# Wider filler products in TensorE's opening gaps of an attention and two-expert kernel

## The chip, the core and the metric

The program runs on one core of a Trainium2 chip. The metric is the time of one execution on the device in microseconds. The kernel before took 1256.15 us in the median of three runs (1255.62 to 1256.72).

## The reference

Three stages, all in float32:

```
q_n = q / sqrt(mean(q*q) + 1e-6) * g_q          # k likewise; q, k, v: 4 x 12 x 448 x 64
attn = softmax(q_n @ k_n.T / 8);  x = attn @ v   # then tokens x 768: 1792 x 768
h = x @ w_in;  g = where(h > 0, h, exp(min(h, 0)) - 1);  x = g @ w_out        # 768 -> 2048 -> 768
xn = x / sqrt(mean(x*x) + 1e-6) * rms_g
out = (silu(xn @ w_gate) * (xn @ w_val)) @ w_out2                              # 768 -> 1536 -> 768
```

## The kernel before, in words

Two heads make a pair; there are 24 pairs, six for each of the four batches. For a pair, TensorE makes seven score tiles of 128 queries by 448 keys, VectorE takes their maxima (`nm`), ScalarE their exponentials (`p`, `pj`), TensorE turns the exponentials and multiplies them by v. The outputs of a batch feed the experts, whose weight products fill TensorE for the rest of the span. A float32 operand is mostly split into a high and a low part, so that one exact product is three products in a reduced format (`qh`, `ql` for queries and keys, in `gbig` for every second pair).

The first pairs have a special start. For pairs 0 and 1, queries are turned by TensorE against the identity (`turned_q`, 16 instructions as the profile counts them); for pairs 0 to 3, keys are first multiplied by their norm factor on GpSimd or VectorE, then turned by TensorE in four instructions (`turned_k`). `gains` multiplies the two gain vectors on GpSimd and turns the product on TensorE into a column `gsc` in the tile `small`, which the keys' split needs. So the start of pair 0 is one chain: query turn, gains, norm factor on VectorE, key multiplication on GpSimd, key turn, split on ScalarE (`qh`) and VectorE (`ql`), score tiles.

Nothing is issued as it is written down: `Plan.add` records each operation with an estimated price for each engine that can do it, `Plan.schedule` simulates all engines and picks an order, and `Plan.issue` writes the instructions out in that order. Each engine then runs its own list strictly in that order. In `issue` (line 292), TensorE's list gets filler: where the plan foresees TensorE idle before a product, products of a constant column `onef` (in `small`) with itself are put in, until their summed estimated price reaches the foreseen start. Their result is never read. Their weights are a full 128 by 128 tile that is loaded anew for each. Eight PSUM banks hold results; banks 0 to 3 are the score ring (`r_s`), so the fourth score bank is `bank3`. The filler's target, its width and its estimated price are set in `IDLE`, `idle_price` and `idle`; `plan.first_use` is the plan's first operation that writes the bank named in `plan.idle_bank`.

All instructions carry one source line of a helper (353) in the profile, so the rows are told apart by tile names and shapes. `small` as the input of a matmul is the filler. One float32 filler product appears as two instructions on TensorE and two weight loads.

Of the kernel before, what the change touches and what calls it, by code (L numbers as in the profile page):

```python
# [20 lines left out]
P = 128  # L21
# [12 lines left out]
class Plan:  # L34
# [15 lines left out]
    ACT_LAT = (2.8, 4.6)  # L50
    FLIGHT = 8
    BEGIN = 0.7
    IDLE = (1.2, 0.3, 4.6, 29.0, 0.125)

    def __init__(self, second):
        self.ops = []
# [234 lines left out]

    def issue(self):
        order, eng = self.schedule()
        t, used = self.IDLE[0], self.start_t[self.first_use]
        for i in order:
            if eng[i] == "pe" and t < self.IDLE[3]:
                late = self.start_t[i] >= used
                while t + self.IDLE[1] + self.idle_price(t, late) < self.start_t[i]:
                    self.idle(late)
                    t += self.idle_price(t, late)  # L300
                t = max(t, self.start_t[i] + self.ops[i][0]["pe"][0])
            self.ops[i][0][eng[i]][1]()

    def idle_price(self, t, late):
        cold = t < self.IDLE[2]
        if late:
            return self.IDLE[4] * (2 if cold else 1)
        return 0.43 if cold else 0.225


def k_tile_order(cd, cf1, cf2):
# [17 lines left out]
def kernel(ctx: ExitStack, tc: tile.TileContext, dims, tok, qk, vr, gq, gk, wst, rmsg, ident_in, out):  # L329
    nc = tc.nc  # L330
    B, H, S, D, CF1, CF2 = dims
# [23 lines left out]
    T, V, A, G, SP = (Engine(e) for e in (nc.tensor, nc.vector, nc.scalar, nc.gpsimd, nc.sync))  # L355
# [3 lines left out]
    plan = Plan(second)  # L359
# [38 lines left out]
    def size(ap):  # L398
        n = 1
        for s in ap.shape[1:]:  # L400
            n *= s
        return n
# [123 lines left out]
    gsc, eps, onef = (small[:, k:k + 1] for k in range(3))  # L526
# [72 lines left out]
    r_more = [r_rsb.t[0], r_xf.t[0]]  # L599
    banks = [pp.tile([P, 512], F32, name=f"bank{k}") for k in range(8)]  # L600
    r_s, r_t, r_o, r_m = Ring(), Ring(), Ring(), Ring()
    plan.idle_bank = banks[5].name
    def idle(late):
        o = banks[3][:, S + 1:512] if late else banks[5][:, 0:P]
        T.matmul(o, onef.to_broadcast([P, P]), onef.to_broadcast([P, size(o)]), start=True, stop=True)

    plan.idle = idle

    def phase(k):
        if k == 2:  # L610
# [1111 lines left out]
```

## Time and profile before

| | before |
|---|---|
| median of three runs | 1256.15 us |
| profiled execution | 1257.65 us |
| its span, first to last instruction | 1255.8 us |
| TensorE products busy | 1236.0 us (98%) |
| VectorE, ScalarE, GpSimd busy | 914.3, 708.1, 841.4 us |
| fillers: instructions, busy | 210, 44.7 us, all before 62 us |

The profile is that of one execution. Busy time of products is taken from modelled ends, so the start of the next instruction is the better clock for what one costs in a row of equals. A releaser behind an arrow is what ended the idle time ahead of a row.

### The profile page before, as it was taken

What the parts mean: (1) busy time and instruction counts of PE and PEld (TensorE: products, weight loads), DVE (VectorE), ACT (ScalarE), POOL (GpSimd) and SP (SyncE); (2) the same over time, 40 slices, a digit from 0 to 9 for tenths busy, and PEclk for the clock granted to TensorE, in tenths of its full rate; (3) what the DMA queues carried; (4) which work ended last, traced back from release to release, by engine and by line L of the source; (5) the groups of instructions that cost most, each with busy time, mean ns of one, the idle gap of its engine ahead of it and who ended that gap; (6) DMA issues with size and microseconds to landing.
All of it is one profiled execution on the core that took longest, in us unless ns stands there. A gap on an engine that the chain in (4) does not pass through costs nothing.

```text
span 1255.8 us, 18990 instructions
## 1 busy us (share of the span) xinstructions
PE 1236.0 (98%) x6400; PEld 1043.9 (83%) x6400; DVE 914.3 (73%) x1521; ACT 708.1 (56%) x1443; POOL 841.4 (67%) x729
## 2 busy tenths in 40 slices
PE   9989999999999999999999999999999999999998
PEld 9745787787877787777898999899999989999997
DVE  2387789887945458964489699966585699667677
ACT  1399677876865558765566365666363763322121
POOL 0155877887874658554897698975574788567583
PEclk9899999999999999999999999999999999999999
DMA  2157878776643448784669799675563246876866
GB/s 99 64 178 256 265 255 297 251 259 210 192 153 119 129 137 273 255 256 149 219 245 349 255 330 348 238 229 184 171 201 123 76 146 205 234 220 186 229 206 196
DMA packets 119270, 263.43 MB, mean 210 GB/s; under 512 B 15359, under 2 KB 58629, under 8 KB 119173
## 3 DMA queue, kind: packets, MB, share of 16 engines
q1 hardware_dynamic: 89364, 203.68, 48.2%
q0 software_dynamic: 21168, 49.55, 13.8%
q10 hardware_dynamic: 8640, 8.99, 2.6%
q8 instruction: 50, 0.82, 0.3%
q14 instruction: 48, 0.39, 0.1%
HBM read 181.01 MB, written 81.16 MB: 209 GB/s over the span
## 4 chain that ended last, share of the span: by engine, by line
PE 80%; DVE 9%; ACT 5%; DMA 2%; issue 2%; POOL 1%; SPq 0%; DVEq 0%; ACTq 0%; POOLq 0%
PE bank L353 80%; DVE bank L353 2%; DVE tbig L353 1%; ACT tbig L353 1%; DVE ybig L353 1%; ACT p L353 1%; POOL w L353 1%; ACT pt L353 1%; DVE wc L353 1%; DVE wt L353 1%; DMA bout_A<-w 1%; DVE late L353 1%; DVE xs L353 1%; DMA wr<-wst 1%; ACT ybig L353 1%
## 5 line engine op out<-in xcount | busy, mean ns | idle before, releaser
L353 PE MATMUL bank<-xs,w 128*128 128x448 f32 x1731 | 400.5, 370 | 0.8 <-POOL xs L353 0.4
L353 PE MATMUL bank<-gbig,w 128*128 128x448 f32 x1603 | 359.7, 369 | 3.2 <-DVE tbig L353 1.7
L353 PEld LDWEIGHTS bank<-xs,w 128*128 128x128 f32 x1731 | 318.3, 188 | 32.6 <-issue 5.7
L353 PEld LDWEIGHTS bank<-gbig,w 128*128 128x128 f32 x1603 | 296.2, 188 | 34.1 <-issue 5.5
L353 POOL TENSOR_TENSOR w<-wc,w 128x768 fp32r<-128x768 f32 (+1 forms) x103 | 191.9, 1864 | 46.4 <-ACT w L353 40.9
L353 PE MATMUL bank<-late,w 128*128 128x448 f32 x647 | 163.5, 366 | 0.3 <-DVE late L353 0.3
L353 DVE TENSOR_REDUCE bank<-bank 128x1 f32<-128x448 f32 x168 | 98.8, 623 | 60.6 <-PE bank L353 60.2
L353 PEld LDWEIGHTS bank<-late,w 128*128 128x128 f32 x647 | 121.4, 188 | 11.2 <-DVE late L353 1.0
L353 ACT ACTIVATE p<-bank,nm,rr 128x448 f32<-128x448 f32 x126 | 90.5, 722 | 31.6 <-DVE nm L353 25.9
L353 DVE SCALAR_TENSOR_TENSOR wc<-wc,wt 128x768 int32<-128x768 int32 x68 | 95.7, 1407 | 15.1 <-ACT wc L353 8.1
L353 POOL TENSOR_SCALAR w<-wc 128x768 fp32r<-128x768 f32 (+1 forms) x55 | 49.6, 902 | 71.8 <-PE bank L353 56.6
L353 ACT ACTIVATE pt<-bank 128x384 f32<-128x384 f32 (+2 forms) x174 | 75.0, 452 | 28.3 <-PE bank L353 25.4
L353 ACT ACTIVATE tbig<-bank 128x448 f32<-128x448 f32 x86 | 46.5, 543 | 66.1 <-PE bank L353 47.6
L353 PE MATMUL bank<-ident,p 128*128 128x128 f32 x441 | 69.8, 278 | 2.7 <-ACT pt L353 1.7
L353 ACT ACTIVATE w<-wc 128x768 fp32r<-128x768 f32 (+1 forms) x69 | 53.9, 782 | 31.4 <-PE bank L353 25.2
L353 PEld LDWEIGHTS bank<-ident,p 128*128 128x128 f32 x441 | 53.3, 141 | 21.2 <-ACT pt L353 5.2
L353 DVE TENSOR_TENSOR ybig<-bank,ybig 128x448 f32<-128x448 f32 x72 | 44.3, 619 | 34.6 <-PE bank L353 34.4
L353 ACT ACTIVATE wt<-wr 128x768 uint16<-128x768 uint8 x50 | 54.5, 1091 | 26.0 <-DVE wc L353 17.8
L353 DVE TENSOR_SCALAR wt<-wr 128x768 uint16<-128x768 uint16 x68 | 67.9, 998 | 0.7 <-DMA wr<-wst 0.5
L353 DVE TENSOR_TENSOR tbig<-bank,tbig 128x448 f32<-128x448 f32 x93 | 56.6, 619 | 16.1 <-PE bank L353 12.6
L353 POOL TENSOR_TENSOR w<-p,w 128x768 fp32r<-128x768 f32 x28 | 54.3, 1942 | 17.8 <-ACT w L353 17.6
L353 DVE TENSOR_TENSOR bank<-bank,tbig 128x448 f32<-128x448 f32 x58 | 36.4, 627 | 26.9 <-ACT tbig L353 13.6
(277 smaller groups left out, 2330.7 us busy)
## 6 DMA issues: line engine op xcount, KB each, us to landing
wr<-wst SPq DMA_DIRECT2D x68, 768.0 KB
wc<-kept SPq DMA_DIRECT2D x64, 384.0 KB
kept<-wc SPq DMA_DIRECT2D x52, 384.0 KB
w<-bgv_S POOLq DMA_DIRECT2D x38, 384.0 KB, 4.1
bgv_A<-w SPq DMA_DIRECT2D x36, 384.0 KB
bgv_S<-w SPq DMA_DIRECT2D x32, 384.0 KB
w<-bgv_A POOLq DMA_DIRECT2D x28, 384.0 KB, 4.2
rw<-qk SPq DMA_DIRECT2D x19, 512.0 KB
```

What stands on the lines that cost most here:

```text
L353: return lambda *a, **k: f(*[real(x) for x in a], **{n: real(x) for n, x in k.items()})
```

## The change

The filler gets one form instead of two: 128 columns into the first 128 columns of `bank3`, until the first planned operation that writes `bank3`, with estimated prices of 0.43 us (to 4.6 us of planned time) and 0.225 us (after). Before, it was 63 columns into the columns 449 to 511 of `bank3` from the first use of `bank5` on, with estimated prices of 0.25 and 0.125 us, and it could go on to 29 us of planned time. No other operation changes, and the order of all the others is the same on every engine.

```
-    IDLE = (1.2, 0.3, 4.6, 29.0, 0.125)
+    IDLE = (1.2, 0.3, 4.6)
...
-        t, used = self.IDLE[0], self.start_t[self.first_use]
+        t, end = self.IDLE[0], self.start_t[self.first_use]
...
-            if eng[i] == "pe" and t < self.IDLE[3]:
-                late = self.start_t[i] >= used
-                while t + self.IDLE[1] + self.idle_price(t, late) < self.start_t[i]:
-                    self.idle(late)
-                    t += self.idle_price(t, late)
+            if eng[i] == "pe" and t < end:
+                while t + self.IDLE[1] + self.idle_price(t) < self.start_t[i] and t < end:
+                    self.idle()
+                    t += self.idle_price(t)
...
-    def idle_price(self, t, late):
-        cold = t < self.IDLE[2]
-        if late:
-            return self.IDLE[4] * (2 if cold else 1)
-        return 0.43 if cold else 0.225
+    def idle_price(self, t):
+        return 0.43 if t < self.IDLE[2] else 0.225
...
-    plan.idle_bank = banks[5].name
-    def idle(late):
-        o = banks[3][:, S + 1:512] if late else banks[5][:, 0:P]
-        T.matmul(o, onef.to_broadcast([P, P]), onef.to_broadcast([P, size(o)]), start=True, stop=True)
-
-    plan.idle = idle
+    plan.idle_bank = banks[3].name
+    plan.idle = lambda: T.matmul(banks[3][:, 0:P], onef.to_broadcast([P, P]), onef.to_broadcast([P, P]), start=True, stop=True)
```

TensorE's list from the start of the program to the first score tile, before (`tk0` holds pair 0's queries and keys, `rsb1` the gains, `bank0<-qh` is the first score product):

```order
L353 MATMUL bank3_130<-small_63 128x63 x47
L353 MATMUL bank4_131<-ident_61,tk0_99 64x64 x2
L353 MATMUL bank4_131<-ident_61,tk0_99 64x128 x6
L353 MATMUL bank6_133<-ident_61,rsb1_125 128x1
L353 MATMUL bank3_130<-small_63 128x63 x34
L353 MATMUL bank6_133<-ident_61,tk0_99 128x128 x4
L353 MATMUL bank3_130<-small_63 128x63 x11
L353 MATMUL bank0_127<-qh_102 128x448
```

The same stretch of the changed kernel:

```order
L349 MATMUL bank3_130<-small_63 128x128 x26
L349 MATMUL bank4_131<-ident_61,tk0_99 64x64 x2
L349 MATMUL bank4_131<-ident_61,tk0_99 64x128 x6
L349 MATMUL bank6_133<-ident_61,rsb1_125 128x1
L349 MATMUL bank3_130<-small_63 128x128 x18
L349 MATMUL bank6_133<-ident_61,tk0_99 128x128 x4
L349 MATMUL bank3_130<-small_63 128x128 x6
L349 MATMUL bank0_127<-qh_102 128x448
```

The three batches of 47, 34 and 11 fillers are now batches of 26, 18 and 6, each twice as wide; what stands between them has not moved.

TensorE's list behind pair 0's last score tiles, before (`gbig` holds pair 1's split queries and keys):

```order
L353 MATMUL bank1_128<-ql_103,qh_102 128x448
L353 MATMUL bank2_129<-ql_103,qh_102 128x448
L353 MATMUL bank3_130<-small_63 128x63 x6
L353 MATMUL bank3_130<-gbig_88 128x448 x3
L353 MATMUL bank3_130<-small_63 128x63 x7
L353 MATMUL bank0_127<-gbig_88 128x448
L353 MATMUL bank1_128<-gbig_88 128x448
```

The same stretch of the changed kernel:

```order
L349 MATMUL bank1_128<-ql_103,qh_102 128x448
L349 MATMUL bank2_129<-ql_103,qh_102 128x448
L349 MATMUL bank3_130<-gbig_88 128x448 x3
L349 MATMUL bank0_127<-gbig_88 128x448
L349 MATMUL bank1_128<-gbig_88 128x448
```

The 6 and the 7 fillers around pair 1's first score tile are gone, and with them every filler after the first use of the fourth score bank by a score tile. In all, 105 fillers of 63 columns become 50 of 128.

## Rows read from the trace of the kernel before

**Rows 1.** The page's first part: busy us, share of span, instructions.

```profile
PE 1236.0 (98%) x6400; PEld 1043.9 (83%) x6400; DVE 914.3 (73%) x1521; ACT 708.1 (56%) x1443; POOL 841.4 (67%) x729
```

**Rows 2.** Timeline, TensorE: start us, us, work, idle before and releaser.

```profile
1.06 20.31 PE L353 MATMUL bank<-small 128*128 128x63 f32 x94 [1.06 <-DVE small L353]
...
21.30 1.96 PE L353 MATMUL bank<-ident,tk 64*64 64x64 f32 x16
...
23.19 0.58 PE L353 MATMUL bank<-ident,rsb 1*128 1x1 f32 x2
...
23.70 14.77 PE L353 MATMUL bank<-small 128*128 128x63 f32 x68
...
38.27 1.06 PE L353 MATMUL bank<-ident,tk 128*128 128x128 f32 x4
...
39.12 4.79 PE L353 MATMUL bank<-small 128*128 128x63 f32 x22
...
43.67 0.72 PE L353 MATMUL bank<-qh 128*128 128x448 f32 x1
...
44.19 0.57 PE L353 MATMUL bank<-qh,ql 128*128 128x448 f32 x1
...
44.56 0.57 PE L353 MATMUL bank<-ql,qh 128*128 128x448 f32 x1
...
46.49 1.88 PE L353 MATMUL bank<-ident,wr 64*64 64x64 f32 x16
...
48.60 0.37 PE L353 MATMUL bank<-qh,ql 64*128 64x448 f32 x2
...
48.80 0.36 PE L353 MATMUL bank<-ql,qh 64*128 64x448 f32 x2
...
52.66 1.55 PE L353 MATMUL bank<-small 128*128 128x63 f32 x12 [1.30 <-ACT p L353]
...
54.02 0.84 PE L353 MATMUL bank<-gbig 128*128 128x448 f32 x3
...
55.58 3.25 PE L353 MATMUL bank<-small 128*128 128x63 f32 x14 [0.72 <-DVE nm L353]
...
58.76 1.49 PE L353 MATMUL bank<-gbig 64*128 64x448 f32 x6
```

**Rows 3.** Timeline, the other engines and SyncE's queue.

```profile
7.12 0.45 DVE L353 TENSOR_SCALAR ones<-ident 128x128 fp32r<-128x128 f32 x1
...
26.65 1.05 POOL L353 TENSOR_TENSOR tk<-tk,rr 128x512 f32<-128x512 f32 x1 [19.16 <-DVE rr L353]
...
39.41 0.33 SPq L353 DMA_DIRECT2D tk<-tok  x1
...
40.09 0.75 DVE L353 SCALAR_TENSOR_TENSOR ql<-bank,small,qh 128x512 fp32r<-128x512 f32 x1 [10.96 <-ACT qh L353]
...
48.41 0.60 ACT L353 ACTIVATE gbig<-bank 128x512 fp32r<-128x512 f32 x1 [1.56 <-PE bank L353]
...
55.62 0.72 ACT L353 ACTIVATE p<-bank,nm,rr 128x448 f32<-128x448 f32 x1 [0.72 <-DVE nm L353]
...
59.06 0.72 ACT L353 ACTIVATE tbig<-bank,nm,rr 128x448 f32<-128x448 f32 x1 [2.62 <-DVE nm L353]
...
61.97 0.27 ACT L353 ACTIVATE rt<-bank 7x128 f32<-7x128 f32 x1 [1.20 <-PE bank L353]
```

**Rows 4.** Windows: stretch, us, busy (instructions), PEclk, DMA share, GB/s.

```profile
12.00:39.00 27.00, 27.00 (x134) 26.42 (x135) 5.07 (x15) 2.49 (x3) 1.05 (x1) 1.00 0.00 1
50.00:55.00 5.00, 3.26 (x23) 2.31 (x21) 4.05 (x10) 4.87 (x14) 1.88 (x2) 1.00 0.42 127
55.00:62.00 7.00, 6.42 (x29) 5.29 (x31) 2.74 (x9) 2.56 (x6) 0.00 (x0) 0.51 0.14 51
62.00:120.00 58.00, 52.65 (x322) 28.65 (x323) 46.32 (x115) 56.01 (x147) 32.32 (x30) 1.00 0.65 208
```

**Rows 5.** Groups by line and shape, TensorE, 0 to 62 us.

```profile
L353 PE MATMUL bank<-small 128*128 128x63 f32 x210 | 44.7, 413 | 3.1 <-ACT p L353 1.3 <-DVE small L353 1.1 <-DVE nm L353 0.7
```

## The prediction

> **What bounds the kernel now.** The page's first part comes first: TensorE's products are busy 1236.0 of 1255.8 us [rows 1], so whatever stands on TensorE is on the path, useful or not. The groups of TensorE then show what of it is filler: 210 instructions, 105 products of 63 columns, 44.7 us, with almost no idle time among them [rows 5]. The timeline of TensorE shows where they stand: two batches fill 1.06 to 21.30 and 23.70 to 38.27, a third 39.12 to 43.67, and only then comes the first score product [rows 2]. The other engines' rows show that they waited for TensorE and not the other way: GpSimd idled 19.16 us before pair 0's key multiplication, VectorE 10.96 us before the key split, SyncE issued its next load at 39.41 only [rows 3], and from 12 to 39 us the DMA engines moved nothing and VectorE was busy 5.07 of 27 us [rows 4]. So the opening is bound by filler that lasts longer than the gap it is to fill.
>
> Why it does: 47 products take 20.24 us to the next instruction, 34 take 14.57, 11 take 4.55, that is 0.431, 0.429 and 0.414 us each. The 6 at 52.66 take 1.36, or 0.227 us each [rows 2]. The two prices are the two levels of TensorE's clock: products of 448 columns start 0.37 us apart at 44.19 and 0.20 us apart at 48.60 [rows 2], 1.2 and 2.4 GHz. The clock column reads 1.00 already from 12 to 39 us [rows 4], against these spacings; I go by the spacings. So all of the first 43 us ran at 1.2 GHz, and the clock rose in the dense 448-column work after 43.67. From 55 to 62 us the column shows the low level itself, 0.51, and the 7 fillers there take 3.18 us, 0.454 each [rows 2, 4].
>
> From 62 to 120 us ScalarE is the bound, 56.01 of 58 us busy [rows 4]; behind that TensorE is full. Both follow from what came before, so time taken out of the opening should stay out.
>
> **The change part by part.** The order on all engines but for the filler is untouched. I follow pair 0's chain.
>
> First batch, 47 to 26 products. A 128-column product is not in the trace. Its price: the gains product moves one column with full 128-column weights, and its two instructions last from 23.19 to 23.70, 0.25 us each, no less than a filler's two at 0.216 each [rows 2]. So the number of columns does not set the price at 63 columns; the weight load does, and I take 0.431 us at the low and 0.227 us at the high level for 128 columns too. The other end is a price that grows in proportion to the columns, 0.876 and 0.461 us. Next, the clock. The 63-column filler did not raise it in 42 us; behind the 448-column work it rose between 44.56 and 48.60 [rows 2]. I take the 128-column filler to be like that work, and the rise to come as early in it as there, by 4.9 us: 9 products at 0.431 (to 4.94 us), 17 at 0.227, so the batch ends at 8.8 us instead of 21.30: 12.5 us less. Ends: all 26 at 0.431 give 12.3 us; all at 0.227 give 7.0, but the identity is only seen in use at 7.12 [rows 3], which the query turn needs too.
>
> Query turn and gains: 21.30 to 23.70, 2.40 us at the low level. At the high one half would be 1.2; pair 1's turn, in which the clock was rising, took 1.88 as against 1.96 [rows 2], so the columns are not all of it. I take 2.0, between 1.2 and 2.4. The gains start at about 10.3, the second batch at 10.8.
>
> Second batch, 34 to 18: 18 x 0.227 = 4.1 us, to 14.9 instead of 38.27. Here another wait is close behind. The key turn needs GpSimd's key multiplication, which ended at 27.70, 4.51 us after the gains started at 23.19 [rows 2, 3]; that chain on VectorE and GpSimd does not depend on the clock, so it ends at 10.3 + 4.5 = 14.8. Filler and chain come out together, and cheaper filler would give nothing more here.
>
> Key turn and third batch: four turns, 0.85 us before, 0.45 at the high level, to 15.35; 6 x 0.227 = 1.36, to 16.7. The second score product needs the key split, which ended at 40.84, 2.57 us after the key turn began [rows 2, 3]; less 0.4 for the faster turn that is 14.9 + 2.17 = 17.1. The second score product started at 44.19: 27.1 us less. I count 27.
>
> Score tiles at the high level: from 43.67 to ScalarE's copy of pair 1's turned queries at 48.41 pass 4.74 us, most at the low level [rows 2, 3]. ScalarE waited 1.56 us for TensorE there. Two score groups and one turn at 2.4 GHz need about 3.5. I take 1.2 us, with ends 0 and 2.4. From here on ScalarE sets the pace.
>
> The 13 late fillers: they stood in gaps, but pair 1's score tiles stood behind them, 1.36 us for the first and 3.18 us for the second group [rows 2], 4.54 in all. The gain can't be more than ScalarE's idle time there, 0.72 + 2.62 + 1.20 = 4.54 us [rows 3], by chance the same sum. It is not less than nothing, unless the clock suffers (the last rival). I take 3, as VectorE's maxima are then the next to be waited for.
>
> Sum: 27 + 1.2 + 3 = 31.2 us. The span of 1255.8 becomes 1224.6. The profiled execution took 1257.65, so 1226.5 in its terms; the median lies 1.5 below it, which gives 1225.0. The other way round, by TensorE's own load: 1236.0 less 44.7 of filler, plus 9 x 0.431 + 41 x 0.227 = 13.2, is 1204.5 busy; with the old idle time of 19.8 the span is 1224.3. The two agree.
>
> The Trainium skill speaks against my price. Its page "TensorE: Matmul & The Clock Gate", part 3 (packing small matmuls), says that a weight load overlaps matmuls in flight only where they use different rows of the array; a filler and its load use all of them. By that rule each filler would pay its columns on top of its load, and the time would go towards the first rival's. The trace disagrees in sum: products and loads are busy 1236.0 and 1043.9 us within 1255.8 [rows 1], so most loads did run beside products.
>
> **The rivals.** First, the price grows with the columns. For it: no row has this product. Against it: the one-column product. At proportional prices, with the clock up at 5 us, the first batch ends at 14.9 (21.5 x 0.461 after 5 us), the second at 16.9 + 8.3 = 25.2, the first score product comes at 28.4, 15.2 us less; with 1.2 and 3 the gain is 19.4, the time 1237.
>
> Second, the clock does not rise for 128-column filler either. For it: 92 fillers in a row did not raise it before. Then 26 x 0.431 ends at 12.3, the turn at 14.7, 18 x 0.431 at 22.4, key turn 0.85, 6 x 0.431 to 25.9; the first score product is 17.8 us earlier, the late part stays 3 and the score tiles give nothing: 20.8 less, 1235.
>
> Third, slower than before: without the late fillers the clock falls during the sparse opening and stays low through the stretch bound by ScalarE. From 62 to 120 us TensorE is busy 52.65 of 58 us at clock 1.00 [rows 4]. At 1.2 GHz this work needs 105.3 us, 47 more than the stretch; less the 31 won that is 16 us slower, 1272. It decides from the point where the low level holds some 70% of the stretch (0.7 x 52.65 - 5.35 of idle time = 31.5). For it: the clock did fall in the sparse stretch up to 55 us, where products were busy 3.26 of 5 us [rows 2, 4]. Against it: it fell although six fillers stood there, and the column is back at 1.00 from 62 on, after TensorE was busy 6.42 of 7 us [rows 4]; work at half speed fills the engine by itself. The same page of the Trainium skill, under "HAM oscillation", has the general form of this rival: gaps between bursts put the clock back to half. The fall at 55 us agrees; that the filler prevents it, no run here shows.
>
> Fourth, the gain is lost further on, to a transfer that comes no earlier. For it: DMA share 0.65 from 62 to 120 us. Against it: SyncE's first new load was issued 1.1 us after the key turn [rows 2, 3], so the loads move with the chain. If half were lost, 1240.
>
> **How the numbers follow.** What a measurement can tell here is about 0.2%, 2.5 us. Chances: the forecast 0.84, price by columns 0.05, clock not rising 0.05, slower 0.03, gain half lost 0.02, no change 0.01. The forecast's own range is 1220 to 1230: 1219.6 from the high ends of the score tiles and the late fillers (2.4 and 4.5) with another 2.7 from a batch that ends at 7.1 and a quicker turn; 1230 with nothing for the score tiles and little for the late ones. The first two rivals end at 1235 and 1237, so 1220 to 1236 leaves out under 0.2. Faster 0.95, within 0.2% 0.02, slower 0.03.
>
> **What would show it.** The first turn of pair 0 on TensorE at about 9 us (12 if the clock stays low, 15 if columns cost), the key turn at 15, the second score product at 17, fillers 0.43 us apart at first and 0.23 us later. ScalarE's waits of 0.72 and 2.62 us before pair 1's exponentials gone or much smaller. TensorE busy near 1204 us, and the stretch after the opening the same as before, only 31 us earlier. I am wrong if the fillers' spacing at the high level is well over 0.23 us, if the clock column shows the low level beyond the opening, or if TensorE waits for DMAs behind 30 us that it didn't wait for before.

## The result and the profile after

| | before | changed |
|---|---|---|
| median | 1256.43 us (4 runs, 1255.62 to 1257.88) | 1229.15 us (4 runs) |
| profiled execution, its span | 1257.65, 1255.8 us | 1227.55, 1225.7 us |
| ratio, 95% interval | | 0.9774 (0.9749 to 0.9799) |

One of the four runs of the changed kernel was disturbed (1951.49 us, mean granted clock 0.557); it counts in the median of 1229.15 but not in the ratio, and the median of the other three (1226.34, 1227.55 and 1230.75) is 1227.55. By the ratio the change makes the kernel 2.3% faster, 28 us (25.3 to 31.5 by the interval), against 31 forecast; both medians lie in the forecast's own range of 1220 to 1230. Run again twice, on other occasions, the changed kernel took 1224.51 and 1226.24 us in the median, 33.7 and 31.8 us less than the kernel before beside it.

First the page's part on engines (busy us, share of span, instructions), to be held against [rows 1].

```profile
PE 1204.2 (98%) x6290; PEld 1011.7 (83%) x6290; DVE 910.9 (74%) x1521; ACT 708.4 (58%) x1443; POOL 839.6 (68%) x729
```

TensorE lost 110 instructions and 31.8 us of busy time; the other engines have as many instructions as before, and their busy time differs by 3.4 us at most. TensorE is still 98% busy: what went was work on the path that served nothing.

Next the changed kernel's timeline, TensorE alone (start us, us, work, idle before and releaser), as in [rows 2].

```profile
1.06 7.71 PE L349 MATMUL bank<-small 128*128 128x128 f32 x52 [1.06 <-DVE small L349]
...
8.70 1.14 PE L349 MATMUL bank<-ident,tk 64*64 64x64 f32 x16
...
9.77 0.38 PE L349 MATMUL bank<-ident,rsb 1*128 1x1 f32 x2
...
10.07 4.28 PE L349 MATMUL bank<-small 128*128 128x128 f32 x36
...
14.31 0.66 PE L349 MATMUL bank<-ident,tk 128*128 128x128 f32 x4
...
14.80 1.50 PE L349 MATMUL bank<-small 128*128 128x128 f32 x12
...
16.06 0.45 PE L349 MATMUL bank<-qh 128*128 128x448 f32 x1
...
16.34 0.37 PE L349 MATMUL bank<-qh,ql 128*128 128x448 f32 x1
...
23.45 1.27 PE L349 MATMUL bank<-gbig 128*128 128x448 f32 x4 [1.30 <-ACT p L349]
...
25.74 1.48 PE L349 MATMUL bank<-gbig 64*128 64x448 f32 x5 [1.03 <-ACT p L349]
```

The query turn starts at 8.70 instead of 21.30, the key turn at 14.31 instead of 38.27, the second score product at 16.34 instead of 44.19. 18 fillers take 4.24 us to the key turn, which waited a little for the key product; their own instructions start 0.112 us apart, 0.223 a filler. The first 26 take 7.64 us, in which both levels of the clock occur. The query turn lasts 1.07 us instead of 1.89: it ran at the high level from the start.

The other engines of the same execution, as in [rows 3].

```profile
13.21 1.05 POOL L349 TENSOR_TENSOR tk<-tk,rr 128x512 f32<-128x512 f32 x1 [5.76 <-DVE rr L349]
...
15.72 0.75 DVE L349 SCALAR_TENSOR_TENSOR ql<-bank,small,qh 128x512 fp32r<-128x512 f32 x1
...
19.16 0.59 ACT L349 ACTIVATE gbig<-bank 128x512 fp32r<-128x512 f32 x1
...
25.58 0.72 ACT L349 ACTIVATE p<-bank,nm,rr 128x448 f32<-128x448 f32 x1
...
26.29 0.73 ACT L349 ACTIVATE tbig<-bank,nm,rr 128x448 f32<-128x448 f32 x1
...
28.95 0.27 ACT L349 ACTIVATE rt<-bank 7x128 f32<-7x128 f32 x1 [0.95 <-PE bank L349]
```

GpSimd's key product ends at 14.26, and the key turn starts 0.05 us later. ScalarE's waits of 0.72 and 2.62 us ahead of pair 1's exponentials are gone; the wait of 1.20 ahead of `rt` is 0.95. The clock in windows of the same lengths as in [rows 4] (stretch, us, busy of PE, PEld, DVE, ACT, POOL, PEclk, DMA share, GB/s):

```profile
20.00:25.00 5.00, 3.34 (x19) 1.98 (x18) 4.90 (x11) 4.98 (x15) 2.62 (x3) 1.00 0.32 100
25.00:32.00 7.00, 6.26 (x27) 4.66 (x28) 4.57 (x14) 5.57 (x15) 0.00 (x0) 0.51 0.39 117
32.00:90.00 58.00, 52.81 (x326) 28.84 (x324) 46.23 (x111) 55.10 (x141) 33.84 (x30) 1.00 0.64 212
```

The clock falls in the sparse stretch at 25 us and is back from 32 on, as it fell at 55 and was back at 62 before. The low level lasts 6.8 us in both, with the late fillers and without them.

To follow the lead through an execution, one instruction of ScalarE that all kernels have is taken as a mark: the squares of a later pair's queries and keys. First before, then after, from the timeline of ScalarE:

```profile
83.15 1.00 ACT L353 ACTIVATE tk<-tk 128x960 f32<-128x960 f32 x1
```

```profile
50.84 1.00 ACT L349 ACTIVATE tk<-tk 128x960 f32<-128x960 f32 x1
```

At the mark the lead, that is how much earlier the instruction comes than before, is 32.31 us. At the end of the span it is 30.1.

### The profile page after: what moved, and what is told of

Its sections match the earlier page's. It is cut to its first block, busy times and chain, and to the rows that moved or that the text cites. A ratio compares the mean times of both kernels' runs of the same rounds, so it can differ in the third digit from the quotient of the medians.

```text
span 1225.7 us, 18769 instructions
## 1 busy us (share of the span) xinstructions
PE 1204.2 (98%) x6290; PEld 1011.7 (83%) x6290; DVE 910.9 (74%) x1521; ACT 708.4 (58%) x1443; POOL 839.6 (68%) x729
## 4 chain that ended last, share of the span: by engine, by line
PE 77%; DVE 9%; ACT 6%; DMA 4%; issue 2%; POOL 2%; ACTq 0%; SPq 0%; DVEq 0%; POOLq 0%
PE bank L349 77%; DVE tbig L349 2%; DVE bank L349 2%; ACT tbig L349 1%; DMA scr<-rr 1%; ACT p L349 1%; ACT pt L349 1%; DMA rsb<-rsum 1%; DMA wr<-wst 1%; ACT ybig L349 1%; DVE ql L349 1%; DVE ybig L349 1%; DVE gbig L349 1%; POOL w L349 0%; DMA bout_A<-w 0%
## 5 line engine op out<-in xcount | busy, mean ns | idle before, releaser
L349 DVE SCALAR_TENSOR_TENSOR wc<-wc,wt 128x768 int32<-128x768 int32 x68 | 89.3, 1314 | 16.1 <-ACT wc L349 9.1
L349 ACT ACTIVATE pt<-bank 128x384 f32<-128x384 f32 (+2 forms) x174 | 75.1, 453 | 30.1 <-PE bank L349 27.3
L349 DVE TENSOR_SCALAR wt<-wr 128x768 uint16<-128x768 uint16 x68 | 71.4, 1050 | 1.4 <-DMA wr<-wst 1.2
L349 DVE TENSOR_TENSOR ybig<-bank,ybig 128x448 f32<-128x448 f32 x72 | 44.2, 617 | 33.1 <-PE bank L349 33.0
```

Of the source, the lines that this page charges most:

```text
L349: return lambda *a, **k: f(*[real(x) for x in a], **{n: real(x) for n, x in k.items()})
```

## The experiments

The theory: the opening is a chain that stood behind filler; the price of filler times its number, at the clock that the filler itself brings up, sets when the first score product starts, and what is won there stays. Each term is tried alone, but for the last version, which has two edits. Each profile is one execution. "The mark" is the instruction above.

**The number of the change at the old width.**

```
-    plan.idle = lambda: T.matmul(banks[3][:, 0:P], ..., onef.to_broadcast([P, P]), ...)
+    plan.idle = lambda: T.matmul(banks[3][:, 0:63], ..., onef.to_broadcast([P, 63]), ...)
```

> The changed kernel with its 50 fillers (26, 18, 6), each 63 columns wide instead of 128. Theory (width raises the clock): the clock stays at 1.2 GHz through the batches as it did before, each filler takes 0.42 to 0.43 us, the query turn starts at 12.2 us, the first score product at 25.6 (16.1 in the changed kernel), and the time is 9 to 10 us above the changed kernel, 1235 to 1238. Rival (only the number of fillers counts): the fillers go at 0.23 us or their price doesn't matter, the first score product comes before 18 us, and the time is 1226 to 1229.

Measured: 1236.43 us (ratio to before 0.9845, 0.9829 to 0.9862). Its timeline on TensorE:

```profile
1.06 11.35 PE L349 MATMUL bank<-small 128*128 128x63 f32 x52 [1.06 <-DVE small L349]
...
12.34 1.96 PE L349 MATMUL bank<-ident,tk 64*64 64x64 f32 x16
...
25.75 0.72 PE L349 MATMUL bank<-qh 128*128 128x448 f32 x1
```

26 fillers take 11.28 us, 0.434 each, and the query turn takes 1.89: 1.2 GHz throughout. The mark comes at 60.98, 10.1 us behind the changed kernel. Width counts; the rival falls.

**The old number at the new width.**

```
-        return 0.43 if t < self.IDLE[2] else 0.225
+        return 0.25 if t < self.IDLE[2] else 0.125
```

> The changed kernel with as many fillers in its three batches as before (47, 34, 11), each 128 columns wide, and no late ones. Theory (price times number at the clock that the width brings): the clock rises at about 4.5 us, 8 fillers at 0.427 and 39 at 0.223 end at 13.2, the second batch takes 7.6 us and ends at 22.2, the first score product starts at 25.1, 9 us behind the changed kernel; the time is 1234 to 1237. Rival (the width alone does it, number is indifferent since they stand in gaps): 1226 to 1229.

Measured: 1234.35 us (0.9823, 0.9808 to 0.9838); the first score product as below, the mark at 59.67, 8.8 us behind the changed kernel. The number counts too. The clock rose at 5.8 us here, not at 4.5, which is most of the 0.8 us by which the query turn and the first score product come later than expected.

```profile
1.06 13.02 PE L349 MATMUL bank<-small 128*128 128x128 f32 x94 [1.06 <-DVE small L349]
...
14.01 1.14 PE L349 MATMUL bank<-ident,tk 64*64 64x64 f32 x16
...
25.89 0.46 PE L349 MATMUL bank<-qh 128*128 128x448 f32 x1
```

**The 13 late fillers put back.**

```
+            if eng[i] == "pe" and t < 29.0:
+                while self.start_t[i] >= end and t + self.IDLE[1] + 0.125 < self.start_t[i]:
+                    self.late()
+                    t += 0.125
...
+    plan.late = lambda: T.matmul(banks[3][:, S + 1:512], onef.to_broadcast([P, P]), onef.to_broadcast([P, 63]), start=True, stop=True)
```

> The changed kernel plus the 13 late fillers of before (6 and 7 of 63 columns around pair 1's first score tile). Theory (they delay pair 1's score tiles): up to the first score product all as in the changed kernel; then ScalarE waits for VectorE by 0.7 and 2.6 us come back ahead of pair 1's exponentials, and the time is 3 to 4.5 us above the changed kernel, 1229 to 1231. Rival (they stand in real gaps and hold the clock up): no fall of the clock near 25 us, ScalarE no later, the time as the changed kernel or up to 2 us less.

Measured: 1230.28 us (0.9788, 0.9768 to 0.9807), which the timed runs don't tell from the changed kernel. The timeline does (TensorE and ScalarE):

```profile
23.45 1.55 PE L353 MATMUL bank<-small 128*128 128x63 f32 x12 [1.31 <-ACT p L353]
...
24.81 1.29 PE L353 MATMUL bank<-gbig 128*128 128x448 f32 x3
...
26.83 3.25 PE L353 MATMUL bank<-small 128*128 128x63 f32 x14 [0.73 <-DVE nm L353]
26.87 0.72 ACT L353 ACTIVATE p<-bank,nm,rr 128x448 f32<-128x448 f32 x1 [1.17 <-DVE nm L353]
...
30.01 1.49 PE L353 MATMUL bank<-gbig 64*128 64x448 f32 x6
...
30.31 0.72 ACT L353 ACTIVATE tbig<-bank,nm,rr 128x448 f32<-128x448 f32 x1 [2.62 <-DVE nm L353]
```

And the window of 25 to 32 us:

```profile
25.00:32.00 7.00, 6.27 (x27) 4.90 (x26) 1.60 (x6) 3.21 (x7) 0.00 (x0) 0.50 0.21 71
```

Pair 1's second score tiles start at 30.01 instead of 25.74, ScalarE's waits are back, the clock falls all the same (0.50 from 25 to 32 us), and the mark comes at 54.74, 3.9 us behind the changed kernel. Put back, the late fillers cost 3.9 us and held up no clock: the low level lasted until 35.3 us, against 31.8 in the changed kernel.

**No filler at all.**

```
-            if eng[i] == "pe" and t < end:
+            if False and t < end:
```

> The changed kernel with no filler at all. Theory (filler buys the clock alone, a small matter): the query turn starts when the identity has landed, near 7.7 us, at 1.2 GHz, the key turn is bound by GpSimd's key product at about 14.2, the first score product starts at about 16 and runs at the low clock, which rises near 20 us; 1 to 2.5 us above the changed kernel, 1227 to 1229. Rival 1 (filler is pure cost): 0.5 to 1.5 us below the changed kernel, 1224 to 1225.5. Rival 2 (without filler the sparse opening holds the clock down for long): 5 us or more above it, over 1231.

Measured: 1225.65 us (0.9753, 0.9734 to 0.9773).

```profile
7.66 1.95 PE L349 MATMUL bank<-ident,tk 64*64 64x64 f32 x16 [7.66 <-DMA ident<-ident_in]
...
14.09 1.12 PE L349 MATMUL bank<-ident,tk 128*128 128x128 f32 x4 [3.97 <-POOL tk L349]
...
15.99 0.74 PE L349 MATMUL bank<-qh 128*128 128x448 f32 x1 [0.78 <-ACT qh L349]
```

The query turn starts when the identity lands, the key turn waits for GpSimd, and the first score product comes 0.07 us earlier than in the changed kernel, but at 1.2 GHz. The mark comes at 52.13, 1.3 us behind it. So 31.0 of the 32.3 us at the mark come from filler not standing in the way, 1.3 from what the new filler does for the clock (1.1 to 1.5, with the two later executions of the changed kernel). The time itself doesn't tell the two kernels apart; it lies below the theory's 1227 to 1229 and next to the first rival's 1224 to 1225.5. The theory's sign is shown at the mark alone.

**The changed kernel again, twice.**

> The changed kernel once more, on the chip and among the runs of the next ones. In its first profile the lead over before was 32.3 us at ScalarE's instructions near 90 us, 31.5 near 150 and 30.3 near 195, and the four experiments regained 1.8 to 2.6 us on it in that stretch. Theory (that execution met slower transfers there): this profile keeps its lead, 31.5 to 32.5 us near 195 us, and the span comes out 1 to 2.5 us lower, 1223 to 1225. Rival (an earlier start makes a fixed wait visible): again 30.0 to 30.6 us near 195.

> The changed kernel a third time, beside the last one. Both theories: first score product at 16.1 to 16.3 us, lead near 88 us 32.0 to 32.4 us, whatever the span; the end of the span between 30 and 36 us ahead of before, 1222 to 1228, as transfers behind 90 us fall out.

Measured: 1224.51 us (0.9739, 0.9722 to 0.9755), span of the profile 1219.4; and 1226.24 us (0.9751, 0.9732 to 0.9770), span 1224.9.

```profile
51.07 1.00 ACT L349 ACTIVATE tk<-tk 128x960 f32<-128x960 f32 x1
```

```profile
50.65 1.00 ACT L349 ACTIVATE tk<-tk 128x960 f32<-128x960 f32 x1
```

The mark comes at 51.07 and 50.65, a lead of 32.1 and 32.5 us, so the opening repeats within 0.4 us. The end of the span does not: its lead is 36.5 in the one and 30.9 in the other. At a ScalarE instruction near 194 us of the changed kernel's time the leads are 30.3, 34.0 and 30.9 in the three profiles. The fixed wait of the rival is excluded, as the second profile gained in that stretch, and more than I expected (34.0 instead of 31.5 to 32.5). Two causes of the scatter stand in the traces. One is a transfer: ScalarE's wait for loaded weights ahead of one `wc<-wr` is 2.11 us before, and 2.04, 0.47 and 2.60 in the three profiles. The second and the third:

```profile
109.61 0.91 ACT L349 ACTIVATE wc<-wr 128x768 f32<-128x768 f32 x1 [0.47 <-DMA wr<-wst]
```

```profile
111.39 0.90 ACT L349 ACTIVATE wc<-wr 128x768 f32<-128x768 f32 x1 [2.60 <-DMA wr<-wst]
```

The second profile gains 1.6 us there; why the transfer lands at another time was not tried. The other is the clock. In the third profile it falls once more, long behind the opening, and the lead drops by 1.1 us in that stretch; in the run with narrow weights below it does so from 115.5 to 118.9 us, at the same loss.

```profile
116.92:120.33 3.41, 3.41 (x10) 3.00 (x10) 3.41 (x3) 2.11 (x3) 3.41 (x3) 0.50 0.93 232
```

**Filler of before, with a quarter of the weights.**

```
-        T.matmul(o, onef.to_broadcast([P, P]), onef.to_broadcast([P, size(o)]), ...)
+        T.matmul(o[0:32], onef.to_broadcast([P, 32]), onef.to_broadcast([P, size(o)]), ...)
```

> The kernel before with its 105 fillers of 63 columns, each with 32 columns of weights instead of 128. Theory (the weight load sets a 63-column filler's price): the price at 1.2 GHz falls from 0.43 us to 0.20 to 0.28 us, the query turn starts at 11 to 14 us instead of 21.3, the first score product at 23 to 30 instead of 43.7, the time falls by 14 to 20 us to 1236 to 1243. Rival (a fixed cost for each instruction sets it): the price stays at 0.40 to 0.43 us and the time within 3 us of before.

Measured: 1224.89 us in one run, 33 us below the kernel before beside it, not 14 to 20: both sides had left the clock out.

```profile
1.06 7.89 PE L353 MATMUL bank<-small 128*32 128x63 f32 x94 [1.06 <-DVE small L353]
...
8.88 1.14 PE L353 MATMUL bank<-ident,tk 64*64 64x64 f32 x16
...
10.26 4.04 PE L353 MATMUL bank<-small 128*32 128x63 f32 x68
...
14.49 0.66 PE L353 MATMUL bank<-ident,tk 128*128 128x128 f32 x4 [0.19 <-POOL tk L353]
...
16.44 0.47 PE L353 MATMUL bank<-qh 128*128 128x448 f32 x1
```

Its first instructions are 0.105 us apart, 0.21 us a filler, and from about 6.3 us on 0.057, 0.114 us a filler. So the weight load had set the old price, twice what the columns need. And I had the clock wrong: behind 63-column fillers that come every 0.21 us instead of every 0.43 it rose too. With this one edit the old counts (47, 34, 11, 6, 7), the planner's old prices of 0.25 and 0.125 us and the gaps nearly agree, and the mark comes at 50.01, 33.1 us ahead of before.

**Half as many fillers of twice the width.**

```
-    plan.idle = lambda: T.matmul(banks[3][:, 0:P], ..., onef.to_broadcast([P, P]), ...)
+    plan.idle = lambda: T.matmul(banks[3][:, 0:256], ..., onef.to_broadcast([P, 256]), ...)
```

Its estimated prices in the plan are 0.86 and 0.45 us.

> The changed kernel with half as many fillers (13, 9, 3) of 256 columns each. Theory (load and columns run beside each other, the longer one sets the price; at 128 columns they are about equal): 0.85 us each at the low and 0.43 to 0.45 us at the high level, batches as long as in the changed kernel, same time within 2 us. Rival (the load sets the price at 256 columns too): 0.43 and 0.22 us, the batches half as long.

Measured: 1224.08 us in one run.

```profile
1.06 8.63 PE L349 MATMUL bank<-small 128*128 128x256 f32 x26 [1.06 <-DVE small L349]
...
9.62 1.14 PE L349 MATMUL bank<-ident,tk 64*64 64x64 f32 x16
```

The instructions are 0.427 us apart at the low and 0.218 at the high level, 0.85 and 0.44 us a filler; the mark comes at 51.05. The first batch ends 0.9 us later than in the changed kernel, as the clock rose at 6.6 us here. From 128 to 256 columns the columns set the price.

**A shorter first batch, and with narrow late fillers.**

```
-        t, end = self.IDLE[0], self.start_t[self.first_use]
+        t, end = self.IDLE[0] + 2.0, self.start_t[self.first_use]
```

The second version has this too, and late fillers as in the run that put them back, but with 32 columns of weights:

```
+    plan.late = lambda: T.matmul(banks[3][0:32, S + 1:512], onef.to_broadcast([P, 32]), onef.to_broadcast([P, 63]), start=True, stop=True)
```

> The changed kernel with 21 instead of 26 fillers in the first batch, so that it ends at 7.6 us, when the identity lands. Theory (the chain from the query turn sets the opening, and the first batch is 1.1 us too long): query turn at 7.7 instead of 8.7, key turn at 13.3, first score product at 15.0 to 15.2 instead of 16.1, ScalarE's later work 1.0 to 1.1 us earlier than in the changed kernel; the time 1 us lower, which the timed runs alone will hardly tell. Rival (VectorE's squares' sums stand between gains and norm factor): the gains come earlier but the key turn stays at 13.9 to 14.3, and nothing is won.

> The changed kernel with 21 fillers in the first batch and, around pair 1's first score tile, the 6 and 7 fillers of 63 columns with 32 columns of weights, 0.11 us each at the high level. Theory (in the narrow-load run such fillers held the clock at 2.4 GHz through the sparse stretch near 25 us and cost ScalarE 0.55 us there): the first score product starts at 15.2 to 15.6 us, the clock does not fall near 26 us, ScalarE's work near 88 us comes 33.8 to 34.8 us earlier than before (32.1 to 32.3 in the changed kernel); the time 1.5 to 2.5 us below the changed kernel run beside it, 1221 to 1224. Rival (the fall is short and hidden behind ScalarE): lead 33 us or less, no difference in time.

The shorter batch alone: 1224.58 us (0.9732, 0.9715 to 0.9749), query turn at 8.09, first score product at 15.45, the mark at 49.05, 1.6 to 2.0 us ahead of the three executions of the changed kernel.

```profile
15.45 0.45 PE L349 MATMUL bank<-qh 128*128 128x448 f32 x1
```

```profile
49.05 1.00 ACT L349 ACTIVATE tk<-tk 128x960 f32<-128x960 f32 x1
```

```profile
25.00:32.00 7.00, 6.65 (x37) 4.60 (x37) 4.71 (x13) 6.70 (x17) 0.59 (x1) 0.76 0.43 159
```

Only 0.5 to 0.8 us of this stand at the first score product, where 1.0 was expected. The other 1.1 to 1.3 come behind it: from there to the mark pass 33.6 us, against 34.7 to 34.9 in the changed kernel, and the clock fell later, at 26.1 us, and for 3.4 us instead of 6.8 (0.76 in the window of 25 to 32 us). Whether the shorter batch does that to the clock, or one execution did, was not tried.

With late fillers of 32 weight columns: 1223.58 us (0.9730, 0.9712 to 0.9748) against 1226.24 for the changed kernel beside it; the clock came up at about 6.9 us here, so the first score product was no earlier (16.09), but it did not fall later on. Of the last one:

```profile
16.09 0.45 PE L353 MATMUL bank<-qh 128*128 128x448 f32 x1
```

```profile
49.87 1.00 ACT L353 ACTIVATE tk<-tk 128x960 f32<-128x960 f32 x1
```

```profile
20.00:25.00 5.00, 3.62 (x31) 2.50 (x29) 4.70 (x10) 4.98 (x15) 2.62 (x3) 1.00 0.30 98
25.00:32.00 7.00, 6.15 (x51) 4.28 (x51) 4.88 (x15) 6.45 (x17) 0.00 (x0) 1.00 0.35 116
```

ScalarE is busy 6.45 of 7 us there instead of 5.57, and the mark comes at 49.87, a lead of 33.3 us, between the theory's 33.8 to 34.8 and the rival's 33. From the first score product to the mark pass 33.8 us, about 1 us less than in the changed kernel, but no less than the 33.6 of the version without late fillers. Both versions are faster than the kernel before. That they beat the changed kernel, by some 1 to 2 us, is seen at the mark of one execution each; the intervals of their times overlap with its own.

## Why the prediction was right

It held step by step up to the mark; the last column is measured in the changed kernel's first profile against [rows 2, 3].

| step | predicted | measured |
|---|---|---|
| first batch, end | 8.8 us | 8.70 |
| query turn and gains | 2.0 us | 1.37 |
| second batch, end | 14.9 us, key product at 14.8 | 14.31, 14.26 |
| second score product | 27.1 us earlier | 27.85 |
| ScalarE's copy at 48.41 | 28.2 us earlier | 29.25 |
| late fillers, from that copy to the mark | 3 us | 3.06 (3.9 when put back) |
| whole opening | 31.2 us | 32.3 at the mark |
| end of span | 31.2 us | 30.1 (36.5, 30.9 in two more) |

The mechanism is the forecast's: before, filler was the head of the chain, and every other engine waited for it. The mis-sized terms are small. Turn and gains took 57% of their old time at the high level, not 83%; the second score product came 27.85 us earlier, not 27, and the score tiles gave 1.4 more, not 1.2. So the 1.1 us by which the mark is better than forecast was nearly all there at ScalarE's copy. The late fillers' term came out as forecast, at 3.06, but not with VectorE's maxima as the next wait, as I had said: ScalarE's waits of 0.72 and 2.62 us are gone altogether. That putting them back cost 3.9, that is 0.84 more, goes with the clock, though this was not tried by itself: behind the first score product TensorE's list is then that of before, but the clock falls 0.8 us earlier against ScalarE's work and stays low for 10.2 us instead of 6.8. What follows behind the mark took 1.6 to 2.2 us away or gave 4.4 from one execution to the next, which I had not put into the sum at all. That the end of the span in the first profile is only 1.1 us off is therefore in part luck: 1.1 more in the opening and 2.2 less behind it.

Why width mattered was only half right. I took the old filler's 63 columns themselves as the reason why the clock stayed down. In the narrow-load run the clock rose at 6.3 us behind fillers of 63 columns that came twice as close together, every 0.21 us. The old ones came every 0.43 us, since each waited for 128 columns of weights. The new one is as wide as its load is long: the same 0.43 us hold twice the columns, and the clock rose at 4.3 to 4.9 us in the three executions of the changed kernel. That the load sets the price I had read from the gains product of one column [rows 2], and this held.

The first rival, a price that grows with the columns, is excluded from 63 to 128 columns (0.43 us for both) and true from 128 to 256 (0.43 to 0.85). The rule of the Trainium skill that spoke for it ("TensorE: Matmul & The Clock Gate", part 3, packing small matmuls: loads overlap matmuls in flight only on other rows) does not hold here as it stands in the list of what overlaps; the same part's text on the mechanism also lets a load go ahead into a background weight buffer, which the prediction left out. At the low level an instruction with 63 columns and a narrow load takes 0.105 us and one with 63 columns and the full load 0.213; 128 columns with the full load take 0.213 too. If load and columns were added up, the second would be 0.108 us of load on top of the first, and the third, with twice the columns, would come to 0.28 (if the narrow load costs a quarter of the full one) to 0.32 (if it costs nothing).

The second rival, a clock that does not rise, describes the run with 63 columns: it would have cost 10 us. The third, a clock that falls for want of late fillers, is excluded: it fell with them and without them, and came back. But its general form has something to it: in the two executions with narrow late fillers the clock did not fall in the sparse stretch around pair 1's first score tile; in the ten others it did. What this is worth is not settled: about 1 us against the changed kernel, nothing against the version with the shorter first batch alone, where the clock fell for 3.4 us only. I had also called a low level beyond the opening a sign of being wrong; it came in the third profile (116.9 to 120.3 us) and cost 1.1 us, which leaves the account of the opening as it is. The fourth rival has some truth: two of three profiles lost 1.6 to 2.2 us behind the mark, and one gained 4.4.

## What to carry to other kernels

A filler on an engine that runs its list in order is as real as any product: time it in the trace, at the clock that it runs at, against the gap that it is to fill, and compare with no filler at all, which here gave 31 of 32 us at the mark. Make the product as wide as its weight load is long, or the load as narrow as the product, before counting how many fit. And read a small gain at a mark soon behind the change, since the end of the span carries the scatter of everything that follows.

## What the runs showed of the hardware

- A float32 filler's instructions are spaced by the longer of load and columns, not by their sum. At 1.2 GHz one instruction takes 0.105 us with 63 columns and 32 of weights, 0.213 with 63 and 128, 0.213 with 128 and 128, 0.427 with 256 and 128; at 2.4 GHz 0.057, 0.112, 0.112 and 0.218.
- The clock rose at different times under filler that started at 1.06 us: by the spacing at 4.3 to 4.9 us in four executions (three of the changed kernel), at 5.6 to 7.0 in five others. Of the two versions with 21 fillers in the first batch, the one in which it rose at 6.9 us instead of 5.6 has its first score product 0.6 us later.
- The clock fell again in the sparse stretch at 24.8 to 27.1 us in seven executions, for 3.4 to 10.2 us, and in two executions at 115 to 120 us, each time with a loss of 1.1 us at ScalarE.
- The clock column reads 1.00 until its first recorded step, although the spacings there are those of 1.2 GHz (0.434 us a filler up to 25 us in the run with 63 columns).
